# Two units of linear attention turned by VectorE's block transpose in place of TensorE's, in a fused attention and SwiGLU kernel

## The chip, the cores and the metric

The kernel runs on one core of one Trainium2 chip. Its metric is the device time of one execution in microseconds (us). Before the change that is 597.2 us, the median of three runs (596.88 to 598.33).

An engine is named as the profile names it: PE is TensorE, with PEld for its weight loads, DVE is VectorE, ACT is ScalarE, POOL is GpSimd, and SP is the engine that issues most of the DMAs. "L371" is line 371 of the kernel before the change.

## The reference

Two blocks follow each other. The first is a linear attention with a decaying state (RWKV-5), over 4 batches, 8 heads, 768 tokens and a head size of 48. The second is a SwiGLU feed-forward network over the 3072 tokens that come out, with 384 features and 1536 hidden ones. All is float32.

```python
for t in range(S):
    kt, vt, rt = (k[:, :, t], v[:, :, t], r[:, :, t])
    cur = np.einsum('bhd,bhe->bhde', u[None] * kt, vt)
    y[:, :, t] = np.einsum('bhd,bhde->bhe', rt, state + cur)
    state = w[None, :, :, None] * state + np.einsum('bhd,bhe->bhde', kt, vt)
...
x = y.transpose(0, 2, 1, 3).reshape(B * S, H * D)
g = x @ w_gate
return (g * (1.0 / (1.0 + np.exp(-g))) * (x @ w_val)) @ w_out
```

## The kernel before

**Units.** The attention is cut into 24 units: 6 chunks of 128 tokens for each of 4 batches; unit i is chunk i // 4 of batch i % 4. For one unit, all 8 heads are handled as four pairs. The steps of a unit are:

- `load` and `load_v` (L141, L148): DMAs issued on SP bring k, r and v into SBUF, tokens on partitions.
- `scale_k` and `scale_r` (L329, L332): POOL multiplies k and r by powers of the decay. The results are called khat and rhat. They lie in `hats`, one tile of eight slots of 512 columns (8 heads of 64). Slots 0, 2, 3 and 5 are four khat buffers, 1 and 4 are two rhat buffers, and 7 and 6 are scratch, called `blocks`.
- `own_product` and `own_sum` (L254, L255 on POOL, L260 on DVE), with `diagonal` (L350 on ACT): the token's own term, put on the diagonal of the score matrix `At`.
- the turn: khat and rhat, with tokens on partitions, become kT and rT, with features on partitions. Two ways of doing this are described below.
- `scores` (L423 on PE): the products of kT and rT for each head into two PSUM banks of `ring_a`; `masked_copy` (L433 or L437 on DVE) takes the causal part into `At`. The second of a unit's two masked copies is done at once for a unit below BLOCKS, and otherwise by the next `feed`.
- `outputs` (L476 on PE, L480 on ACT) and `update` (L491 on PE, L503 on DVE, L504 on POOL): the unit's outputs, turned as xT for the network, and the new state.

**The two turns.** A unit below BLOCKS (12 before the change) is turned by `turn`: PE transposes the eight 128 x 128 tiles against an identity (L371) into two PSUM banks, and ACT copies the two banks out (L375; DVE does that for the first four units). A unit from BLOCKS on is turned by `move_blocks` and `turn_blocks`. DVE's transpose works inside 32 x 32 blocks. So 16 DMAs on SP (L386), each from 32 partitions to 32 partitions, first put every block where its transposed form belongs, in hats slots 6 and 7. Then two DVE transposes of 128 x 512 (L401) write kT and rT, with one `feed` between them. There is one scratch area, so the moves of a unit wait for the transposes of the unit before.

From unit 12 on (`SWAPPED`) the second half of the heads also has its tokens exchanged between the two halves of the partitions; L1255 and L1259 prepare the scale tables for that. Which rhat buffer a unit uses changes at BLOCKS too (`rhat_of`): below, the units take turns; from there on, two following units share one, so that the four blocks of khat and of rhat lie next to each other with one step.

**The network.** Its work for pairs of units is cut into items that wait in a list, `todo`. `feed(n)` takes n items out. `gate_value` (L514) makes one twelfth of the hidden layer of a pair. `two_projections` makes 14 items for two pairs, in the order "00 10 01 02 11 04 03 12 05 06 13 14 15 16"; an item "jp" is the product p of pair j in a scheme of seven products (L589). Item 10 has DVE make two sums of hidden values first (L562, L563), item 01 two more (L565, L566). The first product that reads one of these sums is item 02. Later pairs use a scheme with 15 products for 3 x 3 blocks (L770, with L673 and L700 making weight sums on POOL, L727 input sums on DVE, and L794 collecting the results on DVE, ACT and POOL). The output sums of four weight quarters are made by `weight_sum` (L543, on POOL).

**The order.** Nothing is scheduled by a tool: the order of the main loop (L1246 to L1308) is the order on each engine. In step s, unit s + 1 is scaled, unit s is turned, unit s - 1 has its scores, and unit s - 2 its outputs; from step 12 on (LATE) the outputs directly follow the scores. `gaps(s, n)` at five places of a step feeds network items; for steps 4 to 11 the table EARLY says which: "F" feeds one item, "R" makes a weight rounding or a `weight_sum`. From step 12 on each step has a share of the list, with one item less at the second place, which `turn_blocks` feeds instead. In steps called `late`, the scaling of rhat and the next load come after the turn, since two units share an rhat buffer.

Of the kernel before, what the change touches and what calls it, by code (L numbers as in the profile page):

```python
# [15 lines left out]
P = 128  # L16
# [6 lines left out]
def fast(  # L23
# [28 lines left out]
    HP = H // 2  # L52
# [12 lines left out]
    dve, pool, act, pe, sp = nc.vector, nc.gpsimd, nc.scalar, nc.tensor, nc.sync  # L65
# [27 lines left out]
    def next_psum(m, n):  # L93
        t = ring_a[0]
        ring_a.rotate(-1)
        return t[:, 0 : m * n].rearrange("p (a x) -> p a x", a=m)
# [10 lines left out]
    hats = cst.tile([P, 8, H, 64], FP32, name="hats")  # L107
    khat, rhat = [hats[:, n] for n in (0, 2, 3, 5)], [hats[:, n] for n in (1, 4)]
    At = [cst.tile([P, H, P], FP32, name=f"At{i}") for i in range(2)]
    kT = [cst.tile([P, HP, P], FP32, name=f"kT{i}") for i in range(2)]  # L110


    blocks = [hats[:, n].rearrange("p h x -> p (h x)") for n in (7, 6)]

    def rhat_of(i):
        return rhat[i % 2 if i < BLOCKS else i % 4 // 2]

# [6 lines left out]
    SWAPPED = 12  # L124
# [133 lines left out]
    def own_sum(i):  # L258
        dus[i] = three.tile([P, H], FP32, name="du", tag="du")
        dve.tensor_reduce(dus[i][:], rks.pop(i), axis=AX.X, op=ALU.add)  # L260
# [9 lines left out]
    for e in range(2):  # L270
# [3 lines left out]
        out=ub.rearrange("p h d -> p (h d)"),  # L274
        in_=bass.AP(tensor=u.tensor, offset=u.offset, ap=[[0, P], [1, H * D]]),
# [9 lines left out]
    def warm(n):  # L285
# [9 lines left out]
        out=mask[:], in_=mask[:], compare_op=ALU.is_gt, fill=0.0,  # L295
# [11 lines left out]
    for l in range(7):  # L307
        n = 1 << l
# [12 lines left out]
    turned = {}  # L321
    small = deque()

    def at(i, a):

        return HP - 1 - a if i >= BLOCKS and i % 2 == 0 else a

    def scale_k(i):
        pool.tensor_mul(khat[i % 4][:, :, 0:D], raw(i)[0], kscale)  # L329
# [32 lines left out]
    def pair(t, a):  # L362
        return t[:, 2 * a : 2 * a + 2, :].rearrange("p e d -> p (e d)")

    def turn(i):
        kr = khat[i % 4], rhat_of(i)
        tps = [next_psum(HP, P) for _ in kr]
        turned[i] = three.tile([P, HP, P], FP32, name="rT", tag="rT")
        for tp, t, dst, table in zip(tps, kr, (kT[i % 2], turned[i]), (pw[:, :, 1 : P + 1], pv)):
            for a in range(HP):  # L370
                pe.transpose(tp[:, a, :], pair(t, a), ident[:])  # L371
            if i < 4:
                dve.tensor_mul(dst[:], tp[:], table)
            else:
                act.copy(dst[:], tp[:])  # L375

    def move_blocks(i):


        h = hats[:].rearrange("p n h x -> p (n h x)")  # L380
        first, step = ((0, 1), (11, -1), (12, 1), (23, -1))[i % 4]
        for m in range(4):
            for q in range(4):
                src = h[32 * q : 32 * q + 32, P * first + 32 * m : P * first + 32 * m + 1]
                dst = h[32 * m : 32 * m + 32, P * 31 + 32 * q : P * 31 + 32 * q + 1]
                sp.dma_start(  # L386
                    out=bass.AP(
                        tensor=dst.tensor, offset=dst.offset,
                        ap=[list(dst.ap[0]), [-P, 2 * HP], [1, 32]],
                    ),  # L390
                    in_=bass.AP(
                        tensor=src.tensor, offset=src.offset,
                        ap=[list(src.ap[0]), [P * step, 2 * HP], [1, 32]],
                    ),
                )

    def turn_blocks(i):

        turned[i] = three.tile([P, HP, P], FP32, name="rT", tag="rT")
        for dst, src in ((kT[i % 2], blocks[0]), (turned[i], blocks[1])):  # L400
            dve.transpose(dst[:].rearrange("p a t -> p (a t)"), src)  # L401
            if dst is kT[i % 2]:
                feed(1)

# [2 lines left out]
    def scores(i):  # L407
# [33 lines left out]
        lazy.popleft()()  # L441
        if i < BLOCKS:
            lazy.popleft()()
# [665 lines left out]
    def feed(n, pops=1):  # L1109
        for _ in range(n):  # L1110
            ready = [k for k, (need, _) in enumerate(todo) if need <= done["pool"] + len(summed)]
            if ready:
                todo.pop(ready[0])[1]()
            if lazy:
                lazy.popleft()()
            for _ in range(min(pops, len(small))):
                small.popleft()()
# [22 lines left out]
    def gaps(s, n):  # L1140

        if s not in EARLY:
            if n == 0:
                if s < 18:
                    share[0] = min(-(-len(todo) // (4 - (s - 9) % 4)), 14)
                else:
                    share[0] = -(-(len(todo) + (14 if s < 21 else 0)) // max(25 - s, 1))
            feed(share[0] // 5 + (n < share[0] % 5) - (n == 1 and BLOCKS <= s < N))
            return
# [7 lines left out]
                feed(1, 3)  # L1157

    share = [0]
    BLOCKS = 12  # L1160
    LATE = 12
    EARLY = {s: ("" if s < 7 else "R", "F", "R", "F", "RF") for s in range(5, 12)}
    EARLY[4] = ("R", "F", "", "F", "F")
# [82 lines left out]
    for s in range(4, N + 2):  # L1246
        if 4 < s < N:
            own_sum(s)
        late = BLOCKS < s + 1 < N and s % 2 == 0
        if s + 2 == SWAPPED:  # L1250
            halves_of = two.tile([P, H, D], FP32, name="swapped", tag="rk")[:].rearrange(
                "p (n h) d -> p n h d", n=2
            )
            for p, o in ((slice(0, 64), 64), (slice(64, P), -64)):
                sp.dma_start(  # L1255
                    out=halves_of[p], in_=scales[p.start + o : p.stop + o, 1:3, H // 2 : H]
                )
        if s + 1 == SWAPPED:
            pool.tensor_copy(scales[:, 1:3, H // 2 : H], halves_of)  # L1259
        if s + 1 < N:  # L1260
            scale_k(s + 1)
            if not late:
                scale_r(s + 1)
            own_product(s + 1)
            if s + 1 < BLOCKS:
                load_v(s + 1)
            if s + 3 < N and not late:
                load(s + 3)
        if s < BLOCKS:
            turn(s)  # L1270
        gaps(s, 0)
        if 4 <= s - 1 < N:
            while small:
                small.popleft()()
            scores(s - 1)
            if s >= LATE:
                outputs(s - 2)
                update(s - 2)
            gaps(s, 1)
        if BLOCKS <= s < N:  # L1280
            turn_blocks(s)
        if late:
            scale_r(s + 1)
        if BLOCKS <= s + 1 < N:
            move_blocks(s + 1)
            load_v(s + 1)
        if late and s + 3 < N:
            load(s + 3)
        gaps(s, 2)
        if s - 2 >= 4 and (s < LATE or s > N):  # L1290
            outputs(s - 2)
            update(s - 2)
        if s >= 5 and s % 2:
            queue((s - 3) // 2)
        if s < N:
            diagonal(s)
        if s - 2 >= 4:
            gaps(s, 3)
        gaps(s, 4)
        if s == 12:  # L1300

            dve.tensor_tensor(bad, held[:], wcol[:], ALU.not_equal)
            dve.tensor_reduce(badc, bad, axis=AX.X, op=ALU.add)
            dve.memset(ones, 1.0)
            n_ps = next_psum(HP, P)
            pe.matmul(n_ps[0:1, 0, 0:1], badc, ones, start=True, stop=True)
            act.copy(outside, n_ps[0:1, 0, 0:1])
# [433 lines left out]
```

## Time and profile before

One execution was profiled. It took 597.06 us, of which the span from the first to the last instruction is 595.3 us.

| what | value |
|---|---|
| median of three runs | 597.2 us (596.88 to 598.33) |
| the profiled execution's own time | 597.06 us |
| its span | 595.3 us |
| mean granted TensorE clock | 0.998 |
| VectorE busy | 415.5 us, 70% |
| GpSimd busy | 354.1 us, 59% |
| ScalarE busy | 227.3 us, 38% |
| moves (L386) | 192 DMAs, first issued at 121.5 us |
| TensorE transposes (L371) | 96, from 8.4 to 113.2 us |
| VectorE transposes (L401) | 24, from 136.4 to 398.5 us |

Engine shares are of the span. A busy share alone doesn't say what the time hangs on: for that there is the chain of work that ended last, which is followed back from the last instruction, at each step to what released it. In the views in order of time, the first number is the start in us from the span's start and the second the length. In a row of operations, "out<-in" names the tiles and "x8" is how many records were merged; brackets at the end give the engine's idle time before the row and what ended it. Matmul records overlap, because they are pipelined.

### The profile page before, as it was taken

Reading aid. Unit: us, or ns where it says so; the run is one execution under the profiler, and the core shown is the slowest. Engines: PE = TensorE matmul, PEld = TensorE weight load, DVE = VectorE, ACT = ScalarE, POOL = GpSimd, SP = SyncE. Lnnn points to the kernel's source line nnn. Section 1 sums busy time; section 2 is a strip of 40 time slices with the busy share of each in tenths; the row PEclk is TensorE's granted clock in tenths of the full one; section 3 lists DMA queues with packets and bytes.
Section 4 is the critical chain, followed back from the end, with each engine's and each line's share of the span. In section 5 each row is a group of like instructions: output and inputs, shape, how many; then the busy total and the mean of one; then the engine's idle time right before and its main releaser. Section 6 shows DMA issues by size and latency. Waiting matters only on the chain.

```text
span 595.3 us, 13259 instructions
## 1 busy us (share of the span) xinstructions
PE 580.9 (98%) x5256; PEld 523.1 (88%) x5256; DVE 415.5 (70%) x698; ACT 227.3 (38%) x520; POOL 354.1 (59%) x378
## 2 busy tenths in 40 slices
PE   8799999999999999999999999999999999999995
PEld 7688888899888899988899988789988899988895
DVE  6877886269478877478787476879357878377672
ACT  3468886331353422254331344433034320233310
POOL 5789889988999402977700996513678960010600
PEclk9999999999999999999999999999999999999999
DMA  7989893132431323133234333300100000100001
GB/s 167 254 220 251 224 303 74 32 60 56 88 61 23 54 46 73 41 58 63 35 48 82 72 55 54 48 11 3 53 1 1 1 1 1 55 0 1 2 1 58
DMA packets 139831, 40.68 MB, mean 68 GB/s; under 512 B 130160, under 2 KB 133616, under 8 KB 139760
## 3 DMA queue, kind: packets, MB, share of 16 engines
q1 hardware_dynamic: 136592, 35.42, 27.8%
q10 hardware_dynamic: 3168, 4.33, 2.0%
q8 instruction: 43, 0.70, 0.5%
q14 instruction: 28, 0.23, 0.1%
HBM read 28.51 MB, written 4.72 MB: 56 GB/s over the span
## 4 chain that ended last, share of the span: by engine, by line
PE 88%; POOL 3%; DVE 1%; DMA 1%; ACT 1%; issue 0%; SPq 0%; POOLq 0%
PE bank L770 31%; PE bank L589 18%; PE ring L770 13%; PE bank L996 9%; PE bank L514 7%; PE ring L476 6%; PE ring L423 3%; POOL wgv L242 1%; PE ring L491 1%; DMA r_ld<-in_r_dram 1%; PE ring L371 1%; POOL hats L332 1%; DVE hv L794 0%; POOL rk L254 0%; POOL s L700 0%
## 5 line engine op out<-in xcount | busy, mean ns | idle before, releaser
L794 DVE TENSOR_TENSOR hv<-hv,bank 128x512 f32<-128x512 f32 x132 | 88.0, 683 | 29.1 <-PE bank L770 18.7
L514 PE MATMUL bank<-xT,wgv 128*128 128x256 f32 x288 | 66.8, 385 | 0.6 <-ACT xT L480 0.6
L770 PE MATMUL bank<-xf,wgv 128*128 128x256 f32 x256 | 66.0, 382 | 0.0
L350 ACT ACTIVATE At<-ident,du 128x128 f32<-128x128 f32 x176 | 60.4, 398 | 14.3 <-DVE hv L602 5.9
L794 ACT COPY hv<-bank 128x512 f32<-128x512 f32 x72 | 40.2, 586 | 60.7 <-PE bank L770 54.3
L700 POOL TENSOR_TENSOR s<-wgv 128x256 f32<-128x256 f32 x39 | 30.0, 792 | 52.3 <-PE bank L589 52.1
L514 PEld LDWEIGHTS bank<-xT,wgv 128*128 128x128 f32 x288 | 53.2, 190 | 8.9 <-ACT xT L480 0.9
L770 PEld LDWEIGHTS bank<-xf,wgv 128*128 128x128 f32 x256 | 47.8, 190 | 7.0 <-DVE kT L1038 0.6
L1047 POOL TENSOR_TENSOR hv<-At,hats 128x512 f32<-128x512 f32 x8 | 10.2, 1273 | 66.0 <-ACT At L1046 66.0
L801 ACT ACTIVATE hv<-hv 128x512 f32<-128x512 f32 (+1 forms) x33 | 21.1, 667 | 48.3 <-DVE hv L794 48.3
L770 PE MATMUL bank<-xT,s 128*128 128x256 f32 x152 | 35.5, 380 | 1.0 <-POOL s L700 1.0
L476 PE MATMUL ring<-At,v_ld 128*32 128x128 f32 x768 | 34.9, 273 | 1.5 <-DMA v_ld<-in_v_dram 1.5
L504 POOL TENSOR_TENSOR Z<-Z,w 48x192 f32<-48x192 f32 x32 | 16.6, 520 | 32.1 <-DVE Z L503 30.9
L770 PE MATMUL bank<-xT,wgv 128*128 128x256 f32 x144 | 35.6, 380 | 0.0
L589 PE MATMUL bank<-wt,hs 128*128 128x192 f32 x192 | 33.6, 327 | 0.6 <-DVE hs L563 0.6
L589 PE MATMUL bank<-wo,hs 128*128 128x192 f32 x192 | 34.0, 327 | 0.0
L770 PEld LDWEIGHTS bank<-xT,s 128*128 128x128 f32 x152 | 28.6, 190 | 5.7 <-POOL s L700 1.3
L589 PE MATMUL bank<-wo,hv 128*128 128x192 f32 x192 | 33.3, 328 | 0.0
L589 PEld LDWEIGHTS bank<-wt,hs 128*128 128x128 f32 x192 | 31.4, 190 | 1.3 <-ACT At L350 0.8
L476 PEld LDWEIGHTS ring<-At,v_ld 128*32 128x32 f32 x768 | 30.3, 110 | 2.5 <-DVE At L433 2.3
L589 PEld LDWEIGHTS bank<-wo,hv 128*128 128x128 f32 x192 | 31.5, 190 | 0.5
L589 PEld LDWEIGHTS bank<-wo,hs 128*128 128x128 f32 x192 | 31.6, 190 | 0.3
(218 smaller groups left out, 1394.7 us busy)
## 6 DMA issues: line engine op xcount, KB each, us to landing
hats<-hats SPq DMA_DIRECT2D x192, 32.0 KB, 2.0
w_bits<-in_moe_w_gate_dram SPq DMA_DIRECT2D x6, 768.0 KB, 6.1
w_bits<-in_moe_w_val_dram SPq DMA_DIRECT2D x6, 768.0 KB, 6.0
w_bits<-in_moe_w_out_dram SPq DMA_DIRECT2D x6, 768.0 KB, 6.5
out_dram<-hv ACTq DMA_DIRECT2D x22, 192.0 KB, 2.0
v_ld<-in_v_dram SPq DMA_DIRECT2D x24, 96.0 KB, 5.1
k_ld<-in_k_dram SPq DMA_DIRECT2D x8, 192.0 KB, 3.6
r_ld<-in_r_dram SPq DMA_DIRECT2D x8, 192.0 KB, 4.1
```

The lines of the kernel that those rows point to most:

```text
L350: lambda h=h: act.activation(At[i % 2][:, h, :], ident[:], AF.Identity, scale=du[:, h : h + 1])
L423: pe.matmul(ps[e][keys, a, cols], kT[i % 2][rows, at(i, a), keys], turned[i][rows, at(i, a), cols], start=True, stop=True, skip_group_chec ...
L476: pe.matmul(ps[32 * q : 32 * q + 32, cc, :], *x, start=start, stop=stop, skip_group_check=True,)
L504: pool.tensor_mul(ze, ze, w)
L514: pe.matmul(gv[:, o, :].rearrange("p (i t) -> p i t", i=2), wt[:, c, P * f : P * (f + 1)], xT[:, 2 * g % NX : 2 * g % NX + 2, c, :], start ...
L589: pe.matmul(ps, lhs[:, f, :], rhs[:, f, :], start=(f == 0 and n in (0, 1, 4)), stop=(f == FH - 1), skip_group_check=True,)
L700: op(made[o], made[a], made[b])
L770: pe.matmul(ps[:, o], u[:, o], v, start=first and o == 0, stop=True, skip_group_check=True,)
L794: do(out, *(pair_of(wide[a][:]) if isinstance(a, str) else a for a in args))
L801: todo.append((at, lambda: act.activation(gate, gate, AF.Silu)))
L996: pe.matmul(ps, (h[what][q] if h[what] is D_ else h[what][:, q])[:, f, :], wide["o"][what][:, f, :], start=first and f == 0 and (split or ...
L1047: todo.append((muls, lambda: on.tensor_mul(h, sg, value)))
```

## The change

BLOCKS goes from 12 to 10, so units 10 and 11 are turned by DVE as well. Their turn has a form of its own, for units below SWAPPED: four moves of all 128 partitions each instead of sixteen of 32, and two transposes whose output is written with a step of four elements. The four tokens 4t to 4t + 3 that come together in one row of the scratch area are told apart again by that step.

```diff
     def at(i, a):
-        return HP - 1 - a if i >= BLOCKS and i % 2 == 0 else a
+        return HP - 1 - a if i >= BLOCKS and i % 2 == (i < SWAPPED) else a
...
         first, step = ((0, 1), (11, -1), (12, 1), (23, -1))[i % 4]
+        if i < SWAPPED:
+            for m in range(4):
+                src = h[:, P * first + 32 * m : P * first + 32 * m + 1]
+                sp.dma_start(
+                    out=h[32 * m : 32 * m + 32, 24 * P : 32 * P],
+                    in_=bass.AP(
+                        tensor=src.tensor, offset=src.offset,
+                        ap=[list(src.ap[0]), [P * step, 2 * HP], [1, 32]],
+                    ),
+                )
+            return
...
-        for dst, src in ((kT[i % 2], blocks[0]), (turned[i], blocks[1])):
-            dve.transpose(dst[:].rearrange("p a t -> p (a t)"), src)
+        merged = hats[:, 6:8].rearrange("p n h x -> p (n h x)").rearrange(
+            "p (q n a x) -> p n q a x", q=4, n=2, a=HP
+        )
+        for n, (dst, src) in enumerate(((kT[i % 2], blocks[0]), (turned[i], blocks[1]))):
+            if i < SWAPPED:
+                dve.transpose(dst[:].rearrange("p a (t q) -> p q a t", q=4), merged[:, n])
+            else:
+                dve.transpose(dst[:].rearrange("p a t -> p (a t)"), src)
...
-    BLOCKS = 12
+    BLOCKS = 10
...
+        if s + 1 == BLOCKS:
+            turn(s)
         if s + 1 < N:
             scale_k(s + 1)
...
-        if s < BLOCKS:
+        if s + 1 < BLOCKS:
             turn(s)
```

Other things hang on BLOCKS and move with it:

- Units 10 and 11 share one rhat buffer, the second one, which unit 9 also used. Therefore `turn(9)` is now called ahead of the scaling of unit 10, and step 10 is a `late` step: the scaling of unit 11's rhat comes after `turn_blocks(10)`, and so do `load_v(11)` and `load(13)`, after the moves. `load_v(10)` comes after the moves of unit 10.
- `turn_blocks(10)` and `turn_blocks(11)` feed one network item each, in addition to what EARLY gives. The network is therefore two items ahead from there on, until the shares of later steps even this out. On PE the order of the work is again as before from the scores of unit 17 on.
- The second masked copy of units 10 and 11 waits for the next `feed`.

## The prediction

> **What bounds the kernel now.** I read the busy shares first, then the chain of work that ended last, then the engines that the change touches. Page, busy times, and the head of the chain:
>
> ```profile
> PE 580.9 (98%) x5256; PEld 523.1 (88%) x5256; DVE 415.5 (70%) x698; ACT 227.3 (38%) x520; POOL 354.1 (59%) x378
> PE 88%; POOL 3%; DVE 1%; DMA 1%; ACT 1%; issue 0%; SPq 0%; POOLq 0%
> ```
>
> TensorE holds 88% of the chain. What matters is whether it holds the chain where units 10 and 11 are turned. The chain in order of time (start us, us, what):
>
> ```profile
> 100.44 0.87 PE ring L371 x8
> 101.31 1.09 PE ring L423 x16
> 102.41 2.79 PE bank L514 x12
> 105.19 1.68 PE ring L476 x56
> 106.87 0.34 PE ring L491 x32
> 107.21 5.38 PE bank L514 x24
> 112.59 0.87 PE ring L371 x8
> 113.46 1.09 PE ring L423 x16
> 114.55 2.79 PE bank L514 x12
> 117.34 1.68 PE ring L476 x56
> 119.02 0.34 PE ring L491 x32
> 119.36 2.79 PE bank L514 x12
> 122.14 7.80 PE bank L589 x48
> 129.95 1.09 PE ring L423 x16
> ```
>
> Each piece begins where the one before ends, so TensorE never waits here; the two L371 pieces are units 10 and 11. What leaves TensorE leaves the time, unless a wait takes its place.
>
> The rows for turning, by line (duration ns min/median/max), and the moves (KB each, us to landing):
>
> ```profile
> L371 PE MATMUL ring<-ident,hats x96: 272/273/329, 8.4 to 113.2; 128*128 128x128 f32 x96
> L375 ACT COPY kT<-ring x8: 568/578/595, 42.7 to 113.8; 128x512 f32<-128x512 f32 x8
> L401 DVE STREAM_TRANSPOSE rT<-hats x12: 670/693/718, 141.6 to 398.5; 128x512 f32<-128x512 f32 x12
> hats<-hats SPq DMA_DIRECT2D x192, 32.0 KB, 2.0
> ```
>
> The reader is to see that 273 ns is the length of one pipelined transpose, not its price: eight cost 0.87 us of chain, 0.109 each. Near the change VectorE has this to do (timeline):
>
> ```profile
> 122.60 0.42 DVE L521 TENSOR_TENSOR hv<-sgs,bank 128x256 f32<-128x256 f32 x1 [2.40 <-ACT sgs L520]
> 122.94 0.55 DVE L260 TENSOR_REDUCE du<-rk 128x8 f32<-128x384 f32 x1
> 123.40 1.65 DVE L562 TENSOR_TENSOR hs<-hv 128x768 f32<-128x768 f32 x1
> 125.09 1.64 DVE L563 TENSOR_TENSOR hs<-hs,hv 128x768 f32<-128x768 f32 x1
> ```
>
> It idles 2.40 us before L521, so it has room; but L563 makes the operand that the fourth projection piece (L589) needs.
>
> [...] no strided transpose is in this trace.[...] L562 takes 1.65 us at 123.40 beside GpSimd, 0.95 at the median.[...]
>
> **The change, part by part.**
>
> *Removed from TensorE:* two times eight transposes, 2 x 0.87 = 1.74 us, all on the chain. The scores behind them cost 1.09 whether a turn precedes them (101.31) or not (129.95), so there is nothing more to win. *Removed from ACT:* four copies, 4 x 0.58 = 2.3 us. ACT is 38% busy and the diagonals behind them come sooner; off the path, worth nothing.
>
> *Added to SP and the DMA engines:* eight moves of 128 KB. A unit's four have as many runs of 128 bytes (4096) as the sixteen of a later unit. Sixteen keep the DMA engines 0.32 busy over 121.5 to 134, some 4 us with all else. Issue is 0.61 us each, 2.4 a unit. One lands in 2.0 us at least (the 32 KB row) and 4.1 at most (the 192 KB r load); I take 3. Unit 10's follow the load that ends at 96.1, and land near 101.5, with VectorE coming for them near 105. Unit 11's wait for VectorE's second transpose of unit 10, whose feed item must run in between: near 108.3. They land near 113.8; VectorE comes near 119.9. Both hidden.
>
> *Moved on SP:* load_v(10) from 84.6 to some 99, load_v(11) from 98.2 to some 111, load(13) from 104 to some 112. They are due at outputs 10 and 11 (after 131) and at GpSimd's scaling of unit 13 (122.28); load(13) has landed by 119. load(14) still waits for unit 12's own product (117.5), so unit 12's sixteen moves still start near 121.5. *Moved on GpSimd:* scale_r(10) now waits for TensorE's turn(9), finished at 89.2, and runs at 90.3: no wait. scale_r(11) goes behind own_product(11) and one weight sum, to some 106.6; it waits for unit 10's moves, long landed. Behind it are weight sums due after 122. Nothing.
>
> *Added to VectorE:* four transposes. Dense ones take 0.69. I call the strided one T and take 0.8: the same 512 elements per partition, a penalty of unknown size. Low end 0.69: fewer elements it cannot be. High end 2.8:[...] Queued behind the waiting transpose are L521, which frees a bank, and the L503 pair.
>
> *Moved on TensorE:* the two feed items in turn_blocks pull FFN work forward by two items. By the built order and the pieces above, TensorE then runs: 100.44 scores 9; 101.53 two gate items (5.48); 107.01 outputs and update 8 (2.02); 109.03 two gate items (5.38); 114.41 scores 10; 115.50 a gate item (2.79); 118.29 the first projection piece (1.95); 120.24 outputs and update 9; 122.26 two pieces (3.90); 126.16 the fourth piece, which needs L563. Before, it began at 122.14 + 3 x 1.95 = 127.99, and L563 was done at 126.73: 1.26 to spare. Now L562 stands behind L503 of update 9, which cannot start before 122.35 (L503 followed the end of its update by 0.09). With 0.74 for the pair and some overlap, L562 starts at 123.0, L563 at 124.7, and ends at 126.33; TensorE resumed 0.14 after L563 where it waited for it at 405.15. So 126.47 against 126.16: **0.3 us comes back as a wait**. Bounds: 0, if GpSimd leaves the two alone (0.95 each, done at 125.0); 0.5, if both are as slow as seen plus jitter. The transposes of unit 11 run before that L503: L521 done at 119.2 (0.88 after its matmuls, as before), the masked copy 0.74, so they span 119.85 to 119.85 + 2T = 121.5. Free up to T = 1.25; beyond that they delay the fourth piece by 2T - 2.5.
>
> *Later:* the order of TensorE's work is as before from the scores of unit 17 on, so its waits there stay: 1.1 us at 374.99, behind SP's 12.3 us of moves, and 0.7 at 405.29. In between, scale_r(13) goes behind three of GpSimd's L700, which wait for TensorE: done at 146.7 instead of 143.0. Unit 13's moves (10.5 us) land near 159.2, and VectorE comes near 162. Covered, 2.8 us to spare.
>
> *Sum:* -1.74 + 0.3 = -1.44. The profiled execution took 597.06 us, span 595.3 and 1.8 around it; the median shown is 597.20, 0.14 above. 597.06 - 1.44 = 595.6, or 595.8 on the median's scale; I say 595.7.
>
> **Rivals.**
> *No wait at all* (0.27): L562 and L563 run undisturbed; 597.2 - 1.74 = 595.5. For it: 0.95 is the usual duration. Against: GpSimd's in-place forms (L673) follow at once.
> *A wait further on* (0.16): unit 13's moves are issued in 12.3 us as at 357.94, the spare 2.8 us goes, and VectorE stalls with banks behind it. Price: that of the same pattern at 374.99, 1.1 us; 595.8 + 1.1 = 596.9. Against it: the margin must go first.
> *The strided write is slow* (0.12), the one that ends slower: all of it at unit 11's two transposes, ahead of L503 and L562. Net is -1.44 + 2T - 2.5, zero at T = 1.97. At T = 2.8 it is +1.66: 598.9.[...]
> *My forecast* (0.45): 595.7.
>
> **How the numbers follow.** About 0.3% (1.8 us) is what a measurement of this kernel can tell from no change: faster means below 595.4, slower above 599.0. My full gain, 1.74, lies just at the edge. Faster: most of the no-wait case and a quarter of the forecast's, 0.36. Slower by that much needs a T above 2.8 (that end is an estimate), or the wait further on several times over: 0.08 of those two cases. Same: 0.56. The range goes from 594.9 (no wait, and half a microsecond for the baseline's spread) to 597.3 (the wait further on); the slow write is left out.
>
> **What would show it.** L371 in 80 records instead of 96; both 0.87 pieces gone from the chain; transposes of units 10 and 11 near 0.7 to 0.9 us and waiting for no DMA; a gap of some 0.3 us before the fourth projection piece, put down to L563; no new wait before 280. Wrong if the transposes exceed 1.3 us, if VectorE waits for moves of units 10, 11 or 13, or if TensorE shows new idle time at L770.

## The result, and the profile after

The changed kernel takes **596.35 us** (median of 22 runs, 595.22 to 598.7); the kernel before, run beside it, 597.73 us (22 runs, 596.56 to 599.67). The ratio is 0.9977, with a 95% interval of 0.9968 to 0.9986: some 1.4 us faster, by the interval 0.8 to 1.9. The execution that was profiled took 595.55 us, its span 593.8, the mean granted TensorE clock 0.998.

Lines of the changed kernel lie 17 further down from the scores on: L423 became L440, L491 became L508, L503 and L504 became L520 and L521, L562 and L563 became L579 and L580, L589 became L606. The new moves are L385, the old ones L397; the transpose with a step is L416, the dense one L418.

The page, busy times and the head of the chain that ended last:

```profile
PE 580.3 (98%) x5240; PEld 521.9 (88%) x5240; DVE 421.8 (71%) x702; ACT 225.3 (38%) x516; POOL 355.0 (60%) x378
PE 85%; POOL 4%; SPq 2%; DVE 1%; DMA 1%; issue 1%; ACT 1%; POOLq 0%
```

TensorE has 16 instructions less and still holds the chain. The same stretch of the chain in order of time (start us, us, what):

```profile
100.62 1.09 PE ring L440 x16
101.71 5.38 PE bank L531 x24
...
114.48 1.09 PE ring L440 x16
115.57 2.79 PE bank L531 x12
...
122.33 9.95 PE bank L606 x60
132.27 1.09 PE ring L440 x16
```

The two pieces of 0.87 us ahead of the scores are gone (L371 has 80 records, the last at 89.1), and each piece, in the rows left out too, still starts where the last one ended. The row of 60 matmuls from 122.33 holds the fourth projection piece, which is due 3.90 us in, at 126.23; there is no gap ahead of it.

The new moves by line, with the time to landing:

```profile
L385 SPq DMA_DIRECT2D hats<-hats x8: 643/687/1476, 96.2 to 111.6; - x8
...
DMA to landing us min/median/max: 4.3/5.9/6.5
```

And the new transposes by line:

```profile
L416 DVE STREAM_TRANSPOSE kT<-hats x2: 1129/1138/1148, 105.6 to 119.8; 128x512 f32<-128x512 f32 x2
L416 DVE STREAM_TRANSPOSE rT<-hats x2: 1160/1172/1185, 107.9 to 120.8; 128x512 f32<-128x512 f32 x2
```

A move lands after 5.9 us, not 2.0 as one of 32 KB did; a transpose with the step takes 1.14 to 1.17 us, not 0.69. Both are slower than forecast and both are hidden: VectorE waits 0.28 us for the moves, once, and isn't on the chain there.

How much the change itself moved is read from where each unit's scores start on TensorE, after minus before. From unit 17 on the order of TensorE's work is the same in both kernels, so the difference is clean there; units 3 to 8 come ahead of the change, and their difference, read at unit 8, is an offset that the execution has before the change acts (in the run without extra feeds it grows from 0.20 at unit 3 to 1.39 at unit 8).

| scores of unit | before, us | after | changed kernel again | no extra feeds |
|---|---|---|---|---|
| 8 | 89.10 | +0.17 | -0.07 | +1.39 |
| 17 | 281.38 | -1.54 | -1.69 | -0.33 |
| 20 | 348.34 | -1.54 | -1.68 | -0.34 |
| 22 | 390.05 | -2.00 | -2.40 | -1.01 |
| last matmul | 588.92 | -2.00 | -2.40 | -1.01 |

From unit 8 to units 17 to 20 it is -1.54 - 0.17 = -1.71 (then -1.62 and -1.72): the 1.74 us of the two turns, whole. The two other columns are the first and the third experiment.

A wait of TensorE is counted here from the start of one matmul to the start of the next, less their usual distance. Where it stands in a view's brackets it is some 0.15 us less, because the profile models where a matmul ends.

### The profile page after: what moved, and what is told of

Its sections match the earlier page's. It is cut to its first block, busy times and chain, and to the rows that moved or that the text cites. A ratio compares the mean times of both kernels' runs of the same rounds, so it can differ in the third digit from the quotient of the medians.

```text
span 593.8 us, 13239 instructions
## 1 busy us (share of the span) xinstructions
PE 580.3 (98%) x5240; PEld 521.9 (88%) x5240; DVE 421.8 (71%) x702; ACT 225.3 (38%) x516; POOL 355.0 (60%) x378
## 4 chain that ended last, share of the span: by engine, by line
PE 85%; POOL 4%; SPq 2%; DVE 1%; DMA 1%; issue 1%; ACT 1%; POOLq 0%
PE bank L787 28%; PE bank L606 18%; PE ring L787 13%; PE bank L1013 9%; PE bank L531 7%; PE ring L493 5%; PE ring L440 3%; SPq L397 2%; POOL wgv L242 1%; POOL s L717 1%; PE ring L508 1%; DMA r_ld<-in_r_dram 1%; POOL hats L332 1%; PE ring L371 0%; DVE hv L811 0%
## 5 line engine op out<-in xcount | busy, mean ns | idle before, releaser
L811 DVE TENSOR_TENSOR hv<-hv,bank 128x512 f32<-128x512 f32 x132 | 87.1, 681 | 25.7 <-PE bank L787 14.6
L811 ACT COPY hv<-bank 128x512 f32<-128x512 f32 x72 | 40.1, 585 | 58.6 <-PE bank L787 52.3
L521 POOL TENSOR_TENSOR Z<-Z,w 48x192 f32<-48x192 f32 x32 | 16.8, 526 | 36.7 <-DVE Z L520 35.5
L606 PE MATMUL bank<-wt,hs 128*128 128x192 f32 x192 | 33.7, 328 | 0.6 <-DVE hs L580 0.6
L606 PE MATMUL bank<-wo,hs 128*128 128x192 f32 x192 | 33.9, 327 | 0.0
L606 PE MATMUL bank<-wo,hv 128*128 128x192 f32 x192 | 33.4, 327 | 0.0
L606 PEld LDWEIGHTS bank<-wt,hs 128*128 128x128 f32 x192 | 31.3, 190 | 1.4 <-ACT At L350 0.8
L606 PEld LDWEIGHTS bank<-wo,hv 128*128 128x128 f32 x192 | 31.6, 190 | 0.4
L606 PEld LDWEIGHTS bank<-wo,hs 128*128 128x128 f32 x192 | 31.6, 190 | 0.3
```

The costliest lines, as they stand in the source:

```text
L521: pool.tensor_mul(ze, ze, w)
L606: pe.matmul(ps, lhs[:, f, :], rhs[:, f, :], start=(f == 0 and n in (0, 1, 4)), stop=(f == FH - 1), skip_group_check=True,)
L811: do(out, *(pair_of(wide[a][:]) if isinstance(a, str) else a for a in args))
```

## The experiments

Theory: the gain is the two turns' 1.74 us of TensorE's chain and nothing else, and the rest of the change is hidden. Rivals: part of the gain comes from other order (the two extra feeds, the loads and the scaling moved), or it was lost and given back somewhere; and hidden costs are near to coming out.

**The changed kernel again.** No edit. It tells how far a single profile can be read.

> The changed kernel as it is, timed again on the chip that also runs the next three, so that they can be set against it. Theory (two turns of 0.87 us each leave TensorE's chain, and the four transposes and eight moves are all hidden): in the profile every scores from unit 17 to unit 20 starts 1.7 us earlier than before; time 1.4 to 1.7 us below before. Rival (the 0.46 us that TensorE gained after unit 20, and the 0.5 us that the tail behind the last matmul lost, belong to the change): both come again. If they are chance, they differ here.

Measured: 595.35 us (8 runs) against 596.89 (44 runs), ratio 0.9967 (0.9951 to 0.9983). Scores as in the table. The same gain in the same place. What the rival had named came again as well: between units 20 and 22 TensorE gained a further 0.72 us on the kernel before (0.46 in the first execution), and 6.9 us lay behind the last matmul in both, for 6.40 before. By the test that I had set, this run does not show the two to be chance. It does show that the wait there is not the same from one execution to the next: the first execution waited 0.31 us at 361.28 and 0.26 at 372.98, this one nowhere near there for 0.25.

**TensorE's turns put back.** VectorE still turns the two units, but TensorE also makes sixteen transposes of the identity for each of them at the old place, which nothing uses:

```diff
+        if BLOCKS <= s < SWAPPED:
+            for tp in [next_psum(HP, P) for _ in range(2)]:
+                for a in range(HP):
+                    pe.transpose(tp[:, a, :], ident[:], ident[:])
```

> The changed kernel with sixteen idle transposes put back on TensorE where the two turns stood; their results are not read, so the outputs are the reference's. Theory: the whole gain goes, scores 17 to 20 start within 0.2 us of the kernel before, time within 0.3 us of before. Rival (the gain is from ACT's four copies that are gone, or from the network's work coming two items earlier): the time stays 1.4 to 1.7 us below before.

Measured: 597.29 us (22 runs), ratio 1.0003 (0.9993 to 1.0012). The scores of units 17 to 20 start 0.20 after those of before, with an offset of 0.08. The whole gain is gone, although ScalarE's four copies are gone here too and the network is two items ahead, so it was TensorE's 1.74 us and nothing that came along. Here the wait near 375 us was 1.99 us, longer than in the kernel before.

**No extra feeds.** `turn_blocks` feeds no item for units 10 and 11:

```diff
-            if dst is kT[i % 2]:
+            if dst is kT[i % 2] and i >= SWAPPED:
                 feed(1)
```

> The changed kernel without the network item that the turns of units 10 and 11 feed: TensorE's order is then that of before without the two turns. Theory: the same 1.7 us, since TensorE is never short of work here. Rival (the two items that come earlier pay, or cost, something of their own): scores 17 to 20 differ from the changed kernel's by more than 0.2 us. VectorE's transposes of unit 10 then come some 2 us earlier, so a wait for the moves of unit 10 may show: up to 1.5 us of VectorE's idle time, which nothing on TensorE feels.

Measured: 595.86 us (21 runs), ratio 0.9976 (0.9964 to 0.9987), scores of units 17 to 20 at -0.33 - 1.39 = -1.72. The two items by which the network runs ahead change nothing.

**A slower transpose.** The second transpose of unit 11 is made four times:

```diff
-                dve.transpose(dst[:].rearrange("p a (t q) -> p q a t", q=4), merged[:, n])
+                for _ in range(4 if (i, n) == (11, 1) else 1):
+                    dve.transpose(dst[:].rearrange("p a (t q) -> p q a t", q=4), merged[:, n])
```

> The changed kernel with the second transpose of unit 11 made four times, one after the other, in the place where the slow-write rival put its cost: the same result, some 3.0 us more of VectorE. VectorE had 0.55 us to spare there, so the update of unit 9 and the sums behind it come 2.45 us later. If the sums then run as undisturbed as in the changed kernel (0.97 and 1.15 us), TensorE waits some 1.6 us ahead of the fourth projection piece. If GpSimd then meets them, as the forecast priced it (1.65 us each), TensorE waits some 2.8 us. In both cases the kernel loses its gain, and scores 17 to 20 move by the wait. If TensorE waits for less than 1 us, the rival's place was wrong.

Measured: 598.89 us (14 runs) against 597.84 (43 runs), ratio 1.0012 (1.0000 to 1.0025). VectorE and then TensorE in order of time (lines are one further down than in the changed kernel):

```profile
121.62 4.68 DVE L417 STREAM_TRANSPOSE rT<-hats 128x512 f32<-128x512 f32 x4
...
127.87 1.15 DVE L581 TENSOR_TENSOR hs<-hs,hv 128x768 f32<-128x768 f32 x1
```

```profile
129.16 2.19 PE L607 MATMUL bank<-wt,hs 128*128 128x192 f32 x12 [1.85 <-DVE hs L581]
```

This is the rival's place, seen: the transposes, then the state update (126.11) and the two sums, of which the second lasts to 129.02, and TensorE waiting for it at the fourth projection piece. The price fits the room that the changed kernel has there. In it the update waited 0.55 us for TensorE behind the transposes, and the second sum ended at 125.39, 0.84 ahead of the piece at 126.23, 0.70 with the 0.14 that TensorE takes to resume: 1.25 in all. Three more transposes are 3.45, and 3.45 - 1.25 = 2.2; the wait is 2.0 by the chain. Some 1.6 had been expected with undisturbed sums, from 3.0 us for the three transposes; the sums took 0.97 and 1.15 as in the changed kernel, and the three took more. So some 1.25 us were to spare at the T of 1.15, and the two transposes could, by this estimate, have taken up to 1.78 each at no cost. The scores of units 17 to 20 come 1.78 - 1.06 = 0.72 late, 2.4 behind the changed kernel's; a second wait of 0.32, ahead of 156.98, is in that.

**GpSimd busy ahead of the sums.** Five additions of 128 x 384 whose result is not used, in step 11:

```diff
+        if s == 11:
+            x = two.tile([P, H, D], FP32, name="idle", tag="rk")[:]
+            x = x.rearrange("p h d -> p (h d)").rearrange("p (f n) -> p f n", n=NH)
+            for _ in range(5):
+                pool.tensor_add(x, w21[:, 0:2], w22[:, 0:2])
```

> The changed kernel with five idle GpSimd additions of 128x384 (results not read) ahead of the outputs of unit 9 in step 11, so that GpSimd is at work before VectorE starts the two sums for the fourth projection piece. Theory (the forecast wait of 0.3 us did not come because VectorE started its sum first and GpSimd had to wait): now the sums take about 1.65 us each and TensorE waits 0.2 to 0.5 us ahead of the fourth piece. Rival (the 0.97 us have another reason): the sums stay near 1 us and TensorE does not wait. Over the whole kernel up to 0.5 us; behind it GpSimd is late, which may add a wait for its weight sums near 154.

Measured: 598.32 us (12 runs), ratio 1.0011 (0.9995 to 1.0028). The additions lie over 122.38 to 129.48, and VectorE's second sum beside them:

```profile
125.31 1.65 DVE L580 TENSOR_TENSOR hs<-hs,hv 128x768 f32<-128x768 f32 x1
```

The first one took 1.30. So they are slowed, but not to twice 1.65, and the wait ahead of the fourth piece stays under 0.2 us (unit 11's scores are 2.34 behind those of before with the offset taken out, against 2.16 in the changed kernel). The 0.2 to 0.5 us that had been expected didn't show even here. What made this kernel slower is further on: TensorE waits 1.88 us ahead of 158.68, for a copy on ScalarE, and 0.82 ahead of 192.60, for VectorE. I had not expected that; the last experiment has the first of these waits again, and its cause.

**The old sixteen moves for units 10 and 11**, with dense transposes:

```diff
-        return HP - 1 - a if i >= BLOCKS and i % 2 == (i < SWAPPED) else a
+        return HP - 1 - a if i >= BLOCKS and i % 2 == 0 else a
...
-        if i < SWAPPED:
+        if False:
...
-            if i < SWAPPED:
+            if False:
```

> Units 10 and 11 turned by VectorE in the form of the later units: sixteen moves of 32 partitions, and dense transposes. It shows what the four wide moves are for. SP needs 10.5 us for a unit instead of 3.2 to 3.8. Unit 10's moves then land near 108.5, and VectorE waits 3 us for them at 105.6; unit 11's start near 112 and land near 124, where VectorE would come near 120: it waits some 4 us ahead of the update of unit 9. Theory: TensorE waits some 3 to 5 us ahead of the fourth piece, and the kernel is 1 to 4 us slower than before. Rival (moves are hidden in either form): 1.4 to 1.7 us faster than before.

Measured: 600.29 us (596.19 to 605.4, 22 runs), ratio 1.0041 (1.0024 to 1.0057). It was run again:

> The same kernel as the one with the old sixteen moves of 32 partitions for units 10 and 11 also, whose median was 600.3 us while the one execution profiled took 596.2. Question: what do its usual executions have that the profiled one had not. Theory (VectorE waits for the moves, and how long depends on their landing): a profiled execution near the median has VectorE waits of over 5 us for moves of units 10 and 11 and TensorE waits of 2 to 6 us from 115 to 140 us. Rival (the loss is later, at moves of units 12 on): the waits near 108 and 122 us are as in the first profile, 3.4 and 2.6 us, and the new time shows after 140 us.

Measured: 599.54 us (596.44 to 601.95, 14 runs) against 597.09 (21 runs), ratio 1.0039 (1.0022 to 1.0056). VectorE at unit 11 in the second profile:

```profile
122.79 0.71 DVE L418 STREAM_TRANSPOSE kT<-hats 128x512 f32<-128x512 f32 x1 [2.55 <-DMA hats<-hats]
```

Sixteen moves keep SP busy for 10.5 to 11.2 us where four take some 3.5, so they land later and VectorE waits for them, for unit 10 as well (3.33). TensorE lost some 0.7 us of the gain by it: with the offsets taken out, units 17 to 20 have -0.97 and -0.99 in place of -1.71. Its waits were 0.50 and 0.43 us, near 127 us, where 3 to 5 had been expected. But the two profiled executions took 596.19 and 596.86 us, near the lowest of their runs, and the medians lie 4.1 and 2.7 us above. What the usual executions have that these two had not is open; that they wait longer for moves is likely, and no trace shows it. What is shown is that the new form with four moves is worth more than its slower transposes cost.

**What the step costs.** Unit 11's transposes write densely here (unit 11's tokens are then in another order), and five more transposes into kT ahead of unit 10's write with steps of 1 and 2 (256 elements a partition) and 1, 2 and 4 (128):

```diff
+            if (i, n) == (10, 0):
+                for step, count in ((1, 256), (2, 256), (1, 128), (2, 128), (4, 128)):
+                    dve.transpose(flat[:, 0 : step * count : step], blocks[0][:, 0:count])
```

> The price of a strided transpose by itself. Unit 11's two transposes write densely in the order in which they read, which puts its tokens in a wrong order, so the outputs of unit 11 are not the reference's. For unit 10, five further transposes (128x256 and 128x128 with steps of 1, 2 and 4) are written ahead of the real one, and overwritten by it. Theory (the 1.14 us come from the write's step of four[...]): unit 11's two take 0.70; a step of 2 costs nothing or little, a step of 4 some 1.6 times the dense one of its size. Rival (the 1.14 us come from the four-part read pattern): unit 11's two take 1.14 and the steps make no difference.

Measured, one execution of 596.84 us. The five by line:

```profile
L418 DVE STREAM_TRANSPOSE kT<-hats x5: 311/425/446, 107.3 to 109.0; 128x128 f32<-128x128 f32 x3, 128x256 f32<-128x256 f32 x2
```

The single records are, in order, 445 and 446 ns (256 elements, steps 1 and 2) and 311, 320 and 425 ns (128 elements, steps 1, 2 and 4). A step of two costs next to nothing (1 ns, and 9 ns). A step of four costs 114 ns for 128 elements, 0.89 ns each. Unit 11's dense ones (697 and 669 ns) read the same scattered source as the strided ones do and take 0.68 us against 1.16, so it is the write's step alone: 0.48 us for 512 elements, 0.93 ns each.

**Two more units (8 and 9).** If each turn is worth 0.87, why not start earlier?

```diff
-    BLOCKS = 10
+    BLOCKS = 8
```

> BLOCKS 8 in place of 10: units 8 and 9 are turned by VectorE too. Theory: two more turns leave the chain, scores 17 to 20 start 3.4 us earlier than before, time 3.0 to 3.5 us below before. Rival (in steps 8 and 9 the weights are still loaded and rounded, DMA engines are 0.5 busy and VectorE and GpSimd are nearly full, so the moves and transposes are not hidden): less than 2 us below before, with TensorE waiting in those steps for VectorE or a DMA.

Measured: 613.42 us (5 runs), ratio 1.0283 (1.0257 to 1.0309). What I expected was wrong, the sign too. SP's waits, then those of the other engines, from 60 to 112 us (us in total, times, longest):

```profile
SPq L385 <- DVE rT L416: 10.8, 1, 10.8
```

```profile
DVE wo L214 <- ACT bank L199: 14.4, 4, 7.3
ACT bank L199 <- DMA w_bits<-in_moe_w_out_dram: 13.3, 3, 7.5
...
PE bank L531 <- DVE hv L538: 8.0, 2, 4.5
```

Read from below: TensorE waits for VectorE, VectorE waits for ScalarE's rounding of weights (L199), and that waits for weights to arrive. They are late because SP issues in order. Unit 9's moves wait on SP for VectorE's transposes of unit 8, since there is one scratch area, and the last two weight loads stand behind them: they are issued at 100.17 us, where the changed kernel has issued its last by 84.7. Three more runs take this apart.

**Unit 9 alone more**, `BLOCKS = 9`:

> Three units are turned by VectorE in the new form (9, 10 and 11) instead of two. Theory (what counts is only the turn that leaves TensorE's chain, as long as SP's queue brings the network's weights in time): unit 9 is now the first whose moves stand in SP's queue, so they wait for no earlier transposes, and the last weight loads, at 81 to 84 us, pass as before. One more turn of 0.87 us goes: scores of units 17 to 20 start 2.5 to 2.7 us before those of the kernel before (start-up offset taken out), time 594.2 to 595.3. Rival (each earlier start of the new form costs what the start at unit 8 cost): the weight loads are held up again behind moves, ScalarE waits for w_bits by several us near 85 to 105, and the time is above 600.

Measured: 604.83 us (6 runs) against 597.09 (21 runs), ratio 1.0119 (1.0094 to 1.0143). The theory missed: unit 9's moves wait for no transposes now, but SP needed 7.7 us to issue the four of them from 81.5 on (the single ones 0.8 to 3.8 us, where 0.69 is usual), and the last two weight loads followed at 90.6. TensorE then stood still, and what came next ran slowly; TensorE's timeline, and the row of the ten us behind the wait (us, busy us of PE, PEld, DVE, ACT, POOL, then the granted TensorE clock, DMA share and GB/s):

```profile
100.17 8.35 PE L531 MATMUL bank<-xT,wgv 128*128 128x256 f32 x24 [3.48 <-DVE hv L538]
```

```profile
100.00:110.00 10.00, 9.83 (x42) 7.97 (x43) 6.26 (x13) 3.28 (x11) 4.40 (x6) 0.70 0.92 64
```

The 24 matmuls take 8.35 us where they take 5.45 elsewhere in the same timeline: 2.9 us more, on top of the wait.

**Units 8 and 9, with the last weight loads issued by ScalarE:**

```diff
-            sp.dma_start(
+            (act if n >= 12 else sp).dma_start(
...
-    BLOCKS = 10
+    BLOCKS = 8
```

> The new form from unit 8 on, with the last weight loads (chunks 12 and up) issued by ScalarE instead of SP, so that they can't stand behind unit 9's moves, which wait on SP for VectorE's transposes of unit 8. Theory (the 16.5 us lost with the start at unit 8 came from those two weight loads, issued at 100.2 us instead of 81 to 84): ScalarE's waits for w_bits of 7.5 and 3 us are gone, and four turns of 0.87 leave TensorE's chain: 593.2 to 595. Rival A (the loss comes from the moves and transposes themselves, which VectorE cannot do in time at steps 8 and 9): VectorE's and TensorE's waits near 85 to 110 us stay, time 605 to 613. Rival B (ScalarE now holds the loads up, since it issues them behind its own work, and its rounding is late): in between, 597 to 605.

Measured: 603.71 us (6 runs) against 597.09 (21 runs), ratio 1.0107 (1.0090 to 1.0123). ScalarE's wait for w_bits is gone, and with it 9.9 us of the 16.5 that the same start cost with the loads on SP (6.6 us are left, each against the kernel before on the same chip). So the weight loads were the larger part of that loss, not all. The rest is mostly one wait of TensorE, with its reason on VectorE, and the slow matmuls behind it:

```profile
129.55 4.18 PE L606 MATMUL bank<-wt,hs 128*128 128x192 f32 x12 [5.00 <-DVE hs L580]
```

```profile
123.86 1.10 DVE L416 STREAM_TRANSPOSE kT<-hats 128x512 f32<-128x512 f32 x1 [5.23 <-DMA hats<-hats]
124.81 3.21 DVE L579 TENSOR_TENSOR hs<-hv 128x768 f32<-128x768 f32 x1
```

VectorE waits 3.81 us for unit 10's moves and 5.23 for unit 11's, and the sums stand behind them. Unit 11's moves had waited for unit 10's transposes: the second of these ended at 115.08, and SP issued the moves from 115.14. Unit 10's stood on SP behind the input loads of 98.15 to 103.85. That moves and transposes of units in a row form a chain of their own, slower than TensorE, is thus shown for the last step and likely for the whole. The place is that of the slow-transpose experiment, reached in another way. The rival that named the range (597 to 605) gave another reason for it, loads late on ScalarE, and that was not seen.

**Unit 9, with those loads on ScalarE:** the same edit of the loads, and `BLOCKS = 9`.

> Units 9, 10 and 11 in the new form, and the last six weight loads issued by ScalarE. With the start at 9 on SP the last two loads were issued at 90.6 us, behind unit 9's moves, and TensorE stood still for some 3.7 us; with the start at 8 and the loads on ScalarE the waits for w_bits were gone, but the moves of three following units then followed each other without room, landing 6.4 to 8.8 us after their issue. Theory (both causes are needed for a loss, and the start at 9 with the loads elsewhere has neither: unit 9's moves wait for no transposes, and unit 10's are issued near 96 us, as in the changed kernel): three turns of 0.87 us leave TensorE's chain, scores of units 17 to 20 start 2.4 to 2.7 us earlier than those of the kernel before, time 594.2 to 595.5. Rival (the moves of unit 9 fall into the stretch up to 95 us in which the DMA engines are 0.8 to 0.9 busy, land 8 us after their issue and hold VectorE and unit 10's moves up): a wait of TensorE near 95 to 130 us and a time of 597 to 603.

Measured: 600.55 us (597.99 to 605.04, 9 runs) against 597.15 (14 runs), ratio 1.0053 (1.0024 to 1.0082). The rival's range, but not its place. TensorE waits nowhere up to 154 us, so the three turns are free as far as that. Then it waits 2.38 us (by the brackets) ahead of 156.54 and 1.66 ahead of 160.20, and the granted clock is 0.83 from 150 to 170. The chain in order of time:

```profile
149.34 0.99 POOL hats L332
...
153.06 2.00 DMA hats<-hats
...
155.14 0.34 ACTq L630
...
155.93 0.48 ACT hv L811
...
156.54 2.01 PE bank L787 x4
```

GpSimd (9.53 busy of 10 us from 150 on) scales unit 13's rhat, L332, at 149.34 where it came at 145.94 in the changed kernel (why it is behind was not followed further); SP issues unit 13's moves behind it; the landing of the fifth of them, issued at 153.06, lets ScalarE issue the store of an output (L630); and behind that store, on the same engine, stands the copy (L811) that frees TensorE's bank. A store of outputs has nothing to do with the moves of unit 13. The trace's records say what joins them: the store waits on semaphore 102, the one that this move signals; moves and stores take turns on eight semaphores, 101 to 108. The store ahead of it had been held in the same way: ScalarE was done with its last piece at 149.98, and it went out at 153.75, when the second move (semaphore 107, issued at 151.06) had landed. With GpSimd's idle additions it is the same: L332 at 150.42, two stores held for 2.0 and 2.5 us, the second on semaphore 107, that of the move issued at 154.97, until 157.26. In the changed kernel the store also waits on 107, and that move, issued at 150.49, had landed by 152.5, 0.8 us ahead of what else the store needed (VectorE, 153.3). This is my rival "a wait further on", with less room than I gave it and through another engine. No version of these beats the changed kernel.

## Why the prediction was right

**The 1.74 us, right.** Measured 1.71, 1.62 and 1.72 in three executions; with the turns put back, gone (ratio 1.0003). On the profile's own scale the sum was 595.6, and the profiled execution took 595.55; on the medians the forecast lay 1.5 us below the kernel before, and 1.4 was measured, less than 0.3%, the likeliest case. The agreement is closer than the working was: in the profiled execution a wait that didn't come and three differences that had not been foreseen nearly offset one another (see below). The full 1.71 lies inside the interval of the measured times, too. One of the prediction's odds doesn't follow from its own numbers: it counted most of the case without a wait as faster than 595.4, and priced that case at 595.5.

**The 0.3 us of a new wait, wrong.** The fourth piece did not wait. The step that failed is "L562 stands behind L503 of update 9 ... L563 at 124.7, and ends at 126.33": VectorE's start was right (122.46 and 123.24, for 122.35 and 123.0), the lengths were not. VectorE and GpSimd in the changed kernel:

```profile
122.46 0.74 DVE L520 TENSOR_TENSOR Z<-ring,Z 48x192 f32<-48x192 f32 x2 [0.55 <-PE ring L508]
123.24 0.97 DVE L579 TENSOR_TENSOR hs<-hv 128x768 f32<-128x768 f32 x1
124.24 1.15 DVE L580 TENSOR_TENSOR hs<-hs,hv 128x768 f32<-128x768 f32 x1
```

```profile
122.89 1.68 POOL L521 TENSOR_TENSOR Z<-Z,w 48x192 f32<-48x192 f32 x2 [1.67 <-DVE Z L520]
```

0.97 and 1.15 in place of twice 1.65. The price of 1.65 was taken from another meeting. There, in the kernel before, GpSimd's L254 had started 0.16 us ahead of the sum of 123.40:

```profile
123.24 1.00 POOL L254 TENSOR_TENSOR rk<-r_ld,k_ld 128x384 f32<-128x384 f32 x1
```

Here what runs beside the sums are the two short halves of GpSimd's state update, and of the two instructions in the row of 1.68 the first ends 0.15 us into VectorE's sum, and the second starts 0.23 us after that sum did and takes 1.11 us in place of 0.50: there GpSimd's is the longer one. The single records of the sums in the kernel before and in the changed one (64, of 128 x 768 each) agree to some hundredths. The 43 that start while GpSimd runs nothing take 0.92 to 0.96 us. The 21 that start while one is under way take what is left of that and 0.81 to 0.82 more. The run with units 8 and 9 and ScalarE's loads has it too: the sum starts 0.22 us behind the start of a weight sum of 2.61, and the 2.39 that are left of that and 0.82 make the 3.21 shown above. A price of such a pair is thus not a constant. The prediction held this case as its first rival ("no wait at all"), with 595.5, at 0.27 against 0.45: too low, because the working had not asked which instruction of GpSimd would stand beside the sums.

**T, half right.** I took 0.8 us for the transpose, it is 1.14 to 1.17; the 0.8 was my estimate, and no trace of before has a strided transpose to show it. The same goes for the high end of 2.8, four times the 0.69. What was measured is that a step of two fp32 is free, or nearly (1 and 9 ns more), and that a step of four is not (0.48 us more for 512 elements). The mistake cost nothing, since the bound of 1.25 that I had worked out held, and it turned out to be too tight: with the sums as short as they are, 1.78. The slow-write rival had the right place, as the slow transpose showed. Its decisive point was wrong: by these figures it lay near 2T = 3.55 + 1.74, that is T = 2.65, not at 1.97.

**The moves, wrong but covered.** 3 us to landing, with 4.1 as the upper bound; 4.3 to 6.5 were measured. The step that failed is "4.1 at most (the 192 KB r load)": it took a load from DRAM for a bound of a move inside SBUF, which it is not. The prediction had counted 4096 runs of 128 bytes for a unit's four moves and used that only to say that the work is the same in sum as with sixteen. Those sixteen come over some 11 us and four come over 3, and the four seem to queue behind each other: by the updates of their semaphores, unit 11's, issued at 109.13, 109.82, 110.88 and 111.59, landed at 113.47, 115.13, 116.79 and 118.10. Queueing is not all of it, since the first of them, too, took 4.3 us; no run isolates the rest. Unit 10's were issued at 96.22 and kept VectorE waiting 0.28 us near 105.6; unit 11's were issued from 109.13 to 112.28, and VectorE came at 119.78. The cover that had been reckoned as 3.5 us for unit 10 was used up. A wait of VectorE for moves of unit 10 was one of the prediction's own signs of being wrong; it came, and cost nothing only because VectorE was off the chain there.

**The later steps, right.** GpSimd's scaling for unit 13 ended at 147.1 (146.7 was reckoned), its moves were issued from 147.15 to 157.66, and VectorE began unit 13's transposes at 162.12 without a wait. The rival "a wait further on" did not come. But I reckoned its 2.8 us of spare time at VectorE; ScalarE's store had 0.8, and two experiments that put unit 13's scaling 3.4 and 4.5 us later ran into it.

**Waits near 375 us, taken as fixed, and what stays open.** The prediction kept 1.1 us at 374.99. In the execution after it was 0.57 in two parts, which is most of why unit 22 shows -2.00 and not -1.54; with the same kernel again it was under 0.25, with the turns put back 1.99, without the feeds 0.46, with the slow transpose 1.88. The time behind the last matmul stood against it, 6.89 us for 6.40; it lies between 6.05 and 7.05 in kernels that have the same work there. So both vary more than they differ here. But there is only one profile of the kernel before, and two executions of the changed kernel and the one without feeds all gained there (0.46, 0.72 and 0.67 us from unit 20 to 22), so whether the change has a part in either is open. That the span's -1.51 is so close to the forecast is luck: -1.71 with the offset of 0.17, and then -0.46 and +0.49, which the prediction did not foresee and which offset one another. A gain of 1.7 us has to be read at a place where the order is the same, not at the end.

## What to carry to other kernels

Read a small gain where the order of both kernels is the same again, with the start-up offset taken out, and repeat the profile before giving the rest a cause. Work moved off a full engine is a gain only while each queue that it goes through has room: two turns gave their whole 1.74 us, and a third or fourth gave a loss, first by weight loads stuck behind moves in SP's order, then, in part, by the single scratch area, then by a store that shared a semaphore with moves. Price two instructions that hold each other up, as VectorE's sums and GpSimd's instructions do here, by who starts first, not by a duration from another meeting.

## What was not expected of the hardware

- In this program SP's moves and ScalarE's stores take turns on eight semaphores, and a store waits for the move that had its semaphore before: two stores on ScalarE were held by moves on SP for 2.0 and 2.5 us in one run (GpSimd's idle additions) and for 3.7 and 1.0 in another (unit 9 and the loads on ScalarE), and TensorE behind them for 1.72 and 2.38 (by the brackets).
- A transpose of VectorE that writes fp32 with a step of four takes 0.9 ns more for each element of a partition (1.16 against 0.68 us for 512); with a step of two, next to nothing (446 against 445 ns for 256, 320 against 311 for 128).
- In the changed kernel 128 KB from SBUF to SBUF in runs of 128 bytes land 4.3 to 6.5 us after issue, against 2.0 for 32 KB. Unit 9's, issued from 80 us on while weights are still loaded, landed after 5.4 to 7.2 us with the loads on SP, and after 8.2 to 12.3 with the last of them on ScalarE (DMA share 0.90 to 1.37 in the stretches of five us from 80 to 95). In the same stretch SP needed up to 3.8 and 3.6 us to issue one, in place of 0.69.
- Stalls of TensorE cost more than themselves in three runs (waits by the brackets). With unit 9 alone, after 3.48 us, the granted clock was 0.70 in the next ten (2.9 us lost again); with units 8 and 9 and the loads on ScalarE, after 5.00 us, it was 0.73, with the next 48 matmuls of L606 at 10.93 us in place of 7.80. It was low behind shorter waits too. With unit 9 and the loads on ScalarE the clock is 0.50 from 156.6 on, right behind the wait of 2.38 and before the one of 1.66; with unit 9 alone it is 0.50 behind a wait of 1.62 ahead of 163.86 (first and second row, the last three numbers again clock, DMA share and GB/s):

```profile
156.60:163.40 6.80, 5.14 (x13) 3.64 (x14) 2.29 (x6) 1.12 (x4) 6.57 (x9) 0.50 0.34 54
```

```profile
164.10:167.50 3.40, 3.40 (x9) 2.68 (x10) 0.86 (x2) 0.72 (x2) 3.32 (x5) 0.50 0.35 54
```

  In two other runs it stayed at 1.00: after the wait of 1.85 us ahead of 129.16 with the slow transpose (1.00 from 130 to 150), and after TensorE had been idle for 1.83 of the ten us from 370 on with the turns put back (1.00 from 350 to 400). So the length of a wait alone doesn't decide, and what does was not shown.
